# Double-width conversion chunks, turned tiles right behind the score mixing, and two-bank score copies in a one-core attention and feed-forward kernel

## The chip, the cores and the metric

The kernel runs on one core of a Trainium2 chip. The metric is the device time of one execution in microseconds (us), lower is better. The engines are TensorE (PE; its weight loads are PEld), VectorE (DVE), ScalarE (ACT), GpSimd (POOL) and SyncE (SP), which here issues the transfers.

## What is computed

Attention with heads mixed before and after the softmax ("talking heads"), for 4 batches, 12 heads, 448 rows and 64 columns a head, and behind it a feed-forward layer on 1792 rows of 768 with 2048 hidden columns. The weights `w_in` and `w_out` come as 64-bit floats.

```python
scores = scale * np.matmul(q, k.transpose(0, 1, 3, 2))
scores = np.einsum('bhij,hg->bgij', scores, w_pre)
scores = scores - np.max(scores, axis=-1, keepdims=True)
attn = np.exp(scores)
attn = attn / (np.sum(attn, axis=-1, keepdims=True) + 1e-09)
attn = np.einsum('bhij,hg->bgij', attn, w_post)
x = np.matmul(attn, v)          # then rows of all heads side by side
h = x @ w_in
g = where(h >= 1, h, where(h <= -1, 0, (h + 1) ** 2 / 4))
out = g @ w_out
```

## The kernel before

**Tiles and groups.** Each batch's 448 query rows are cut into tiles of 120, 120, 120 and 88, 16 tiles in all. A tile's rows are cut into blocks of 10 (or 9), so that 10 rows times 12 heads fill 120 partitions, and the blocks of a tile into three groups of 4 (of 3 in the tiles of 88). There are 48 groups. The main loop at the end makes one step for each group, with one or two steps more.

**A step.** Step n works on group n, finishes group n-1, and prepares later tiles:

- `load_s`: SyncE moves the blocks of group n+1 out of the tile's scores `ssb` into tiles `s`, with rows and heads side by side on partitions.
- `pre` (L218): TensorE mixes the heads, `ps_l <- s, wpre`. Every second block is a "split" block, which `split` (L209) has cut into a rounded high part `sh` and a rest `sl` on VectorE, for three fast matmuls; the others run as plain fp32.
- `row_max` (L229) on VectorE, `exps` (L233) on ScalarE with the row sums in `sm`; `norm` (L239) adds 1e-9, takes the reciprocal on VectorE, and GpSimd scales `w_post` by it for each block (`wr`).
- `visit` runs `pv` (L300), the product with the values for an earlier tile, into the pair of banks `ps_q`, and `post_rest`; `post` (L256) mixes the exponentials of group n-1 with `wr` into `ps_a`, and ScalarE copies them to `aT`.
- `trans_k` (L137) and `trans_q` (L154) turn raw keys and queries with TensorE into `ps_k` and `ps_t`; a copy rounds them to the high part (`kh`, `qh`), and VectorE subtracts for the rest (`kl`, `ql`). Queries of a tile are turned in two steps of three; keys of the next batch, two pairs of heads a step, in the three steps 6 to 8, 18 to 20 and 30 to 32.
- `scores` (L167) multiplies queries and keys for a tile that comes later, two pairs of heads in a call: the first pair of heads goes into `ps_q`, the second into two banks of the pool `ps_l`; four copies then bring the four banks to `ssb`, the first bank of each pair on ScalarE, the second on VectorE.

**Banks.** Six banks of accumulation memory rotate under the tag "l" for `ps_l`, `ps_k`, `ps_t`, `ps_r`, `ps_a` and the `ps_s` of `scores`; the pair `ps_q` is one pair only, used by `pv` and `scores` in turn.

**The conversion.** Beside the attention, 64 chunks of the 64-bit weights (128 partitions x 384 numbers) are turned into 32-bit floats. `conv_units` lists the work of a chunk in slots: a load into `wraw`, two ScalarE instructions (`scaled` L366 and `lowest` L372), two VectorE instructions (a shift L375 and the sign L381), one GpSimd add (L385), and a store to `wsd` or `wod`, from which the feed-forward part reads later. Units are spread evenly over steps 2 to 42, some in the middle of a step (ahead of `post`) and the rest at its end:

```python
convs(share * (n - NC + 0.4))
...
convs(share * (n - NC + 1))
```

**The order** is written out by hand (a manual schedule): each engine runs its instructions in the order in which the loop calls them, and the waits between engines follow from tiles and slots. SyncE's queue is in order too. In a step SyncE has `load_s` first, then what the conversion, `load_q`, `load_k`, `load_v` and `store_x` issue.

**The feed-forward part** begins in the last four steps and takes some 421 us. It keeps operands at fixed places in areas of memory ("xa", "xc", "xd"); `TEMP` are two scratch places of `gate` and `SUM` one of `sum_w`.

## Time and profile before

| | us |
|---|---|
| median of 3 runs | 884.15 (883.63 to 886.98) |
| the profiled execution | 888.73 |
| its span, first to last instruction | 887.0 |
| TensorE busy in the span | 861.9 (97%) |
| VectorE busy | 681.5 (77%) |
| ScalarE busy | 553.9 (62%) |
| GpSimd busy | 178.7 (20%) |
| attention part, steps 0 to 43 | 24.32 to 437.12 |

The profile gives each instruction's start and length by engine. TensorE's matmuls are pipelined, and the ends in the profile are modelled, so a busy TensorE can still be slowed; what a step really costs is seen from the start of one step's first `ps_l` matmul to the next one's. Where an engine stood idle, the profile names what released it, and the chain of waits follows the work that ended last back from the end. TensorE's granted clock is full (1.00) in nearly all stretches. The line numbers are those of the kernel above.

### The profile page before, as it was taken

Reading aid. Unit: us, or ns where it says so; the run is one execution under the profiler, and the core shown is the slowest. Engines: PE = TensorE matmul, PEld = TensorE weight load, DVE = VectorE, ACT = ScalarE, POOL = GpSimd, SP = SyncE. Lnnn points to the kernel's source line nnn. Section 1 sums busy time; section 2 is a strip of 40 time slices with the busy share of each in tenths; the row PEclk is TensorE's granted clock in tenths of the full one; section 3 lists DMA queues with packets and bytes.
Section 4 is the critical chain, followed back from the end, with each engine's and each line's share of the span. In section 5 each row is a group of like instructions: output and inputs, shape, how many; then the busy total and the mean of one; then the engine's idle time right before and its main releaser. Section 6 shows DMA issues by size and latency. Waiting matters only on the chain.

```text
span 887.0 us, 20352 instructions
## 1 busy us (share of the span) xinstructions
PE 861.9 (97%) x7850; PEld 732.4 (83%) x7850; DVE 681.5 (77%) x1123; ACT 553.9 (62%) x1208; POOL 178.7 (20%) x253
## 2 busy tenths in 40 slices
PE   8999999999999999999999999999999999999998
PEld 6677678767777766777778788889999999999998
DVE  4887778877788787888668877898667987777853
ACT  4786588766776867687766566676667535433431
POOL 0333344543344344435220000000000000000000
PEclk9999999999999999999999999999999999999999
DMA  6758778976788788686375744674444453124341
GB/s 159 227 180 226 201 224 257 279 209 207 234 235 265 227 208 244 208 259 215 121 229 160 255 167 151 206 224 136 128 126 160 135 187 134 54 64 133 97 135 62
DMA packets 160453, 162.50 MB, mean 183 GB/s; under 512 B 67941, under 2 KB 154085, under 8 KB 160357
## 3 DMA queue, kind: packets, MB, share of 16 engines
q1 hardware_dynamic: 157524, 160.51, 59.2%
q8 instruction: 62, 1.02, 0.5%
q10 hardware_dynamic: 2832, 0.69, 0.4%
q14 instruction: 35, 0.28, 0.1%
HBM read 88.81 MB, written 33.82 MB: 138 GB/s over the span
## 4 chain that ended last, share of the span: by engine, by line
PE 72%; DVE 9%; ACT 9%; DMA 7%; issue 2%; SPq 1%; POOL 0%; DVEq 0%; ACTq 0%
PE ps_f L753 23%; PE ps_f L588 23%; PE ps_a L264 7%; PE ps_l L227 5%; DMA s<-ssb 4%; ACT e L236 4%; PE ps_q L315 3%; PE ps_l L225 3%; PE ps_q L182 2%; DVE ssb L191 2%; PE ps_s L182 2%; DVE wt L381 2%; ACT aT L266 2%; PE ps_r L280 1%; DVE wt L375 1%
## 5 line engine op out<-in xcount | busy, mean ns | idle before, releaser
L247 POOL TENSOR_SCALAR wr<-wpost,rs 120x120 f32<-120x120 f32 x180 | 114.3, 650 | 260.2 <-DVE rs L243 186.6
L236 ACT ACTIVATE e<-ps_l,nm 120x448 f32<-120x448 f32 x180 | 111.8, 632 | 74.6 <-DVE nm L230 74.4
L264 PE MATMUL ps_a<-wr,e 120*64 120x120 f32 (+1 forms) x2160 | 119.2, 266 | 0.2 <-ACT e L236 0.2
L264 PEld LDWEIGHTS ps_a<-wr,e 120*64 120x64 f32 x2160 | 110.1, 137 | 3.3 <-issue 2.6
L736 ACT ACTIVATE sgh_p<-gq_p 128x1024 fp32r<-128x1024 f32 (+1 forms) x56 | 53.2, 952 | 90.5 <-PE ps_f L753 90.3
L230 DVE TENSOR_REDUCE nm<-ps_l 120x1 f32<-120x448 f32 x180 | 100.9, 615 | 4.6 <-PE ps_l L227 3.9
L480 DVE SCALAR_TENSOR_TENSOR wl<-wi,wh 128x768 fp32r<-128x768 f32 x71 | 67.7, 954 | 41.9 <-ACT wh L477 41.3
L227 PE MATMUL ps_l<-s,wpre 120*120 120x448 f32 x196 | 95.3, 570 | 4.2 <-DMA s<-ssb 3.0
L753 PE MATMUL ps_f<-wh,sgh_p 128*128 128x384 f32 x294 | 98.2, 334 | 0.0
L753 PE MATMUL ps_f<-wh,sgl_p 128*128 128x384 f32 x294 | 98.2, 334 | 0.0
L753 PE MATMUL ps_f<-wl,sgh_p 128*128 128x384 f32 x294 | 98.2, 334 | 0.0
L477 ACT ACTIVATE wh<-wi 128x768 fp32r<-128x768 f32 x71 | 59.7, 842 | 58.0 <-DVE wi L700 18.0
L737 DVE TENSOR_TENSOR sgl_p<-gq_p,sgh_p 128x1024 fp32r<-128x1024 f32 (+1 forms) x56 | 60.9, 1089 | 35.7 <-ACT sgh_p L736 35.7
L266 ACT ACTIVATE aT<-ps_a 128x360 f32<-128x360 f32 x180 | 73.5, 502 | 4.6 <-PE ps_a L264 3.0
L385 POOL TENSOR_TENSOR wt<-wt,wk 128x384 int32<-128x384 int32 x64 | 64.4, 1013 | 27.4 <-ACT wk L372 14.4
L214 DVE CAST sh<-s 120x448 fp32r<-120x448 f32 (+1 forms) x82 | 31.1, 379 | 41.0 <-DMA s<-ssb 40.9
L225 PE MATMUL ps_l<-sh,wpre_h 120*120 120x448 f32 (+1 forms) x82 | 58.4, 712 | 1.3 <-DVE ql L165 1.3
L215 DVE TENSOR_TENSOR sl<-s,sh 120x448 fp32r<-120x448 f32 (+1 forms) x82 | 54.1, 660 | 2.8
L753 PEld LDWEIGHTS ps_f<-wh,sgl_p 128*128 128x128 f32 x294 | 55.2, 188 | 0.0
L753 PEld LDWEIGHTS ps_f<-wl,sgh_p 128*128 128x128 f32 x294 | 55.2, 188 | 0.0
L753 PEld LDWEIGHTS ps_f<-wh,sgh_p 128*128 128x128 f32 x294 | 55.2, 188 | 0.0
L315 PE MATMUL ps_q<-aT,v 128*64 128x120 f32 (+1 forms) x960 | 55.2, 264 | 0.0
(237 smaller groups left out, 2002.0 us busy)
## 6 DMA issues: line engine op xcount, KB each, us to landing
s<-ssb SPq DMA_DIRECT2D x172, 210.0 KB
wraw<-in_moe_w_in_dram SPq DMA_DIRECT2D x32, 384.0 KB
wraw<-in_moe_w_out_dram SPq DMA_DIRECT2D x32, 384.0 KB
wi<-wod SPq DMA_DIRECT2D x29, 384.0 KB
wi<-wsd SPq DMA_DIRECT2D x28, 384.0 KB
wsd<-wt SPq DMA_DIRECT2D x32, 192.0 KB
wod<-wt SPq DMA_DIRECT2D x32, 192.0 KB
wi<-wss SPq DMA_DIRECT2D x16, 384.0 KB
```

Source lines behind the costliest of these rows:

```text
L225: nc.tensor.matmul(out=lps[m], lhsT=w[:k], rhs=y[:k], start=(j == 0), stop=(j == 2))
L227: nc.tensor.matmul(out=lps[m], lhsT=wpre[:k], rhs=x[:k], start=True, stop=True)
L230: nc.vector.tensor_reduce(out=nm, in_=lps[m], axis=AX.X, op=ALU.max, negate=True)
L236: nc.scalar.activation(out=e, in_=ps, func=AF.Exp, bias=nm, accum_out=sm[:, j:j + 1])
L247: nc.gpsimd.tensor_scalar_mul(out=w[:, :, :ni], in0=wpost[:, :, :ni], scalar1=rs[:, j:j + 1])
L264: nc.tensor.matmul(out=ps[half[s], r, :ni * H], lhsT=e[:, c0:c0 + 64], rhs=w[:, :, :ni], start=True, stop=True)
L266: nc.scalar.activation(out=a[:, :, :, c:c + ni], in_=ps[:, :, :ni * H].rearrange("q r (h i) -> q r h i", h=H), func=AF.Copy)
L315: nc.tensor.matmul(out=to[m][half[s], :n], lhsT=x[:, 2 * m + s, r * D:(r + 1) * D], rhs=a[:, r, 4 * g + 2 * m + s, :n], start=False, stop= ...
L385: nc.gpsimd.tensor_tensor(out=st["t"], in0=st["t"], in1=st.pop("k"), op=ALU.add)
L480: nc.vector.scalar_tensor_tensor(out=lo, in0=t, scalar=2.0 ** -8, in1=hi.bitcast(F32), op0=ALU.mult, op1=ALU.subtract)
L588: nc.tensor.matmul(out=o, lhsT=u[:, c, k], rhs=x, start=first and r == 0 and m == 0, stop=r == 2 and m == 2, skip_group_check=True)
L753: nc.tensor.matmul(out=o, lhsT=x[:, f, c], rhs=y[:, f % 2, :], start=first and f == 0 and m == 0, stop=hf == 1 and f == 3 and m == 2, skip ...
```

## The change

**The conversion** gets 32 chunks of 768 numbers in place of 64 of 384, one in a step, in the steps of the list `CS`: 2 to 42 without 7 to 9, 19 to 21 and 31 to 33, the steps in which keys are turned. The load of step n+1's chunk is issued in step n behind the query and key loads; ScalarE's `conv_scaled` stands behind the exponentials, the other four instructions (`conv_rest`) behind `post`, and the store of step n-1's chunk behind those. `wraw` has 2 slots for 3, `wt` 3 for 4, `wk` 1 for 2, each of twice the size; `s10` has 8 slots for 10, `sh` and `sl` 2 for 3.

**Turned tiles.** Queries and keys are turned one step number later than before, but right behind `pre` and not behind `post`; their copies come behind the exponentials and `norm`. The high part of the keys is copied by ScalarE throughout. Loads of raw queries and keys go from the end of a step to the place behind the transposes.

**Scores.** VectorE copies the two banks of `ps_q` with one instruction; ScalarE copies the two `ps_s` banks.

**norm**: GpSimd adds the 1e-9. **gate**: `TEMP` and `SUM` lie elsewhere, with a second pair of `TEMP` places for the later gates.

```diff
@@ trans_k
+        def out():
+            hi, lo = kt[b, hp]
+            nc.scalar.activation(out=hi, in_=ps, func=AF.Copy)
+            nc.vector.tensor_tensor(out=lo, in0=ps, in1=hi.bitcast(F32), op=ALU.subtract)
+
         def rest():
             nc.tensor.transpose(out=ps[:, SM:], in_=y, identity=i)
-            hi, lo = kt[b, hp]
-            if b:
-                nc.vector.tensor_copy(out=hi, in_=ps)
-            else:
-                nc.scalar.activation(out=hi, in_=ps, func=AF.Copy)
-            nc.vector.tensor_tensor(out=lo, in0=ps, in1=hi.bitcast(F32), op=ALU.subtract)
+            return out
         return rest
@@ scores
-        for h, x in todo:
-            nc.scalar.activation(out=ssb[t][:n, h, :], in_=x[:n], func=AF.Copy)
-
-        def copies():
-            for h, x in rest:
-                nc.vector.tensor_copy(out=ssb[t][:n, h, :], in_=x[:n])
-        return copies
+        h = 2 * hps[0]
+        nc.vector.tensor_copy(out=ssb[t][:n, h:h + 2, :], in_=wide[:n, :, :S])
+        for s in range(2):
+            nc.scalar.activation(out=ssb[t][:n, 2 * hps[1] + s, :], in_=ps[1][s][:n], func=AF.Copy)
@@ load_s, split
-        x = ap_.tile([KM, S], F32, tag="s10", name="s10", bufs=10)
+        x = ap_.tile([KM, S], F32, tag="s10", name="s10", bufs=8)
-        hi = ap_.tile([KM, S], F32R, tag="sh", name="sh", bufs=3)
-        lo = ap_.tile([KM, S], F32R, tag="sl", name="sl", bufs=3)
+        hi = ap_.tile([KM, S], F32R, tag="sh", name="sh", bufs=2)
+        lo = ap_.tile([KM, S], F32R, tag="sl", name="sl", bufs=2)
@@ norm
-        nc.vector.tensor_scalar_add(out=rs[:, :k], in0=sm[:, :k], scalar1=1e-9)
+        nc.gpsimd.tensor_scalar_add(out=rs[:, :k], in0=sm[:, :k], scalar1=1e-9)
@@ the conversion (convert and conv_units are gone)
+    CS = [n for n in range(2, NG - 5) if not any(x <= n < x + 3 for x in (3 * t - 5 for t, y in enumerate(tiles)
+                                                                          if t and y[1] == 0))]
+    def conv_load(i):
+        craw[i] = qp.tile([128, 2 * CW], I64, tag="wraw", name="wraw", bufs=2)
+        src = conv_ends(i)[0]
+        nc.sync.dma_start(out=craw[i] if i % 2 else craw[i].rearrange("p (k f) -> p k f", f=128), in_=src)
+    def conv_scaled(i):
+        cwt[i] = qp.tile([128, 2 * CW], I32, tag="wt", name="wt", bufs=3)
+        nc.scalar.activation(out=cwt[i].bitcast(F32), in_=halves(i)[1].bitcast(F32), func=AF.Copy,
+                             scale=2.0 ** -111)
+    def conv_rest(i):
+        lo, hi = halves(i)
+        t = cwt[i]
+        k = qp.tile([128, 2 * CW], I32, tag="wk", name="wk", bufs=1)
+        nc.scalar.activation(out=k, in_=lo.bitcast(U32), func=AF.Copy, scale=2.0 ** -29)
+        nc.vector.tensor_single_scalar(out=t, in_=t, scalar=3, op=ALU.logical_shift_left)
+        nc.vector.scalar_tensor_tensor(out=t, in0=hi, scalar=-0x80000000, in1=t,
+                                       op0=ALU.bitwise_and, op1=ALU.bitwise_or)
+        nc.gpsimd.tensor_tensor(out=t, in0=t, in1=k, op=ALU.add)
+    def conv(n, f):
+        if n in CS and CS.index(n) < 2 * NF:
+            f(CS.index(n))
@@ scratch places
-    SUM = ("xd", 29504)
-    TEMP = (("xd", 32576), ("xd", 36672))
+    SUM = ("xd", 37696)
+    TEMP = tuple(tuple(("xd", x + 4096 * i) for i in range(2)) for x in (29504, 30720))
@@ the loop's tables
-                    at.setdefault(3 * t - 6 + g + (t == 2), []).append(lambda t=t, g=g: trans_q(t, g))
+                    w0 = 3 * t - 5 + g + (t == 2)
+                    at.setdefault(w0, []).append(lambda t=t, g=g: trans_q(t, g))
-                        put(3 * t - 7 + hp // 2, lambda nb=nb, hp=hp: load_k(nb, hp))
-                        at.setdefault(3 * t - 6 + hp // 2, []).insert(0, lambda nb=nb, hp=hp: trans_k(nb, hp))
+                        w0 = 3 * t - 5 + hp // 2
+                        mid.setdefault(w0 - 1, []).append(lambda nb=nb, hp=hp: load_k(nb, hp))
+                        at.setdefault(w0, []).insert(hp % 2, lambda nb=nb, hp=hp: trans_k(nb, hp))
@@ the loop
             for m in ms:
                 pre(m)
             nxt = list(groups[n + 1][1::2]) if n + 1 < NG else []
+            turned = [f() for f in [f() for f in at.pop(n, ())]]
+            for f in mid.pop(n, ()):
+                f()
+            conv(n + 1, conv_load)
             for m in ms:
                 row_max(m, nm[:, m - ms[0]:m - ms[0] + 1])
...
-            for f in copies:
-                f()
+            conv(n, conv_scaled)
             if ms:
                 norm(ms, sm)
+            for f in (*turned, *copies):
+                f()
             for m in nxt:
                 split(m)
-            convs(share * (n - NC + 0.4))
             if n == NG:
                 step(0)
             for m in old:
                 post(m)
-            for f in [f() for f in at.pop(n, ())]:
-                if f:
-                    f()
+            conv(n, conv_rest)
+            conv(n - 1, conv_store)
             if not early:
                 for f in visit(n, rests):
                     f()
-            for f in [scores(t, hps) for t, hps in vis.pop(n, ())]:
-                f()
+            for t, hps in vis.pop(n, ()):
+                scores(t, hps)
             for f in late.pop(n, ()):
                 f()
-            convs(share * (n - NC + 1))
```

VectorE where the first keys of the second batch are turned; `sh`/`sl` are splits, `wt` the conversion's shift and sign, `nm` the row maxima. Before, from the end of step 6 to the maxima of step 7:

```order
L375 TENSOR_SCALAR wt<-wt 128x384
L381 SCALAR_TENSOR_TENSOR wt<-wraw,wt 128x384
L165 TENSOR_TENSOR ql<-ps_t,qh 128x360
L148 CAST kh_1236<-ps_k 128x448
L151 TENSOR_TENSOR kl_1237<-ps_k,kh_1236 128x448
L148 CAST kh_1242<-ps_k 128x448
L151 TENSOR_TENSOR kl_1243<-ps_k,kh_1242 128x448
L191 COPY ssb<-ps_q 88x448
L191 COPY ssb<-ps_s_1270 88x448
L375 TENSOR_SCALAR wt<-wt 128x384
L381 SCALAR_TENSOR_TENSOR wt<-wraw,wt 128x384
L230 TENSOR_REDUCE nm<-ps_l 120x1 x4
```

After, step 7 from its maxima to those of step 8:

```order
L222 TENSOR_REDUCE nm<-ps_l 120x1 x4
L206 CAST sh<-s_1233 120x448
L207 TENSOR_TENSOR sl<-s_1233,sh 120x448
L235 RECIPROCAL rs<-rs 120x4
L146 TENSOR_TENSOR kl_1256<-ps_k,kh_1255 128x448
L146 TENSOR_TENSOR kl_1262<-ps_k,kh_1261 128x448
L166 TENSOR_TENSOR ql<-ps_t,qh 128x360
L206 CAST sh<-s_1235 120x448
L207 TENSOR_TENSOR sl<-s_1235,sh 120x448
L183 COPY ssb<-ps_q 88x896
L222 TENSOR_REDUCE nm<-ps_l 120x1 x4
```

The conversion and the casts of `kh` are gone from between two sets of maxima, the subtractions follow the step's own maxima, and one copy of 896 columns takes the place of two.

SyncE, the step that follows. Before, from the store behind step 7's `post` through its end to the loads of the scores `s`:

```order
L412 DMA wsd<-wt 128x384
L125 DMA qraw<-in_q_dram 120x6x64
L115 DMA kraw<-in_k_dram 128x3x64 x2
L116 DMA kraw<-in_k_dram 64x2x64
L115 DMA kraw<-in_k_dram 128x3x64 x2
L116 DMA kraw<-in_k_dram 64x2x64
L347 DMA xd<-xo 768x1x120
L405 DMA wraw<-in_moe_w_in_dram 128x3x128
L412 DMA wsd<-wt 128x384
L206 DMA s_1486<-ssb 120x1x448
```

After, from the query load of step 7 to the first load of step 8:

```order
L124 DMA qraw<-in_q_dram 120x6x64
L114 DMA kraw<-in_k_dram 128x3x64 x2
L115 DMA kraw<-in_k_dram 64x2x64
L114 DMA kraw<-in_k_dram 128x3x64 x2
L115 DMA kraw<-in_k_dram 64x2x64
L380 DMA wsd<-wt 128x2x384
L339 DMA xd<-xo 768x1x120
L198 DMA s_1405<-ssb 120x1x448
```

One store and one load of the conversion have gone from between the key loads and the score loads; the score loads (`s`) now follow the store of `xo`.

VectorE in a step without keys and with a conversion. Before, step 5 from the reciprocal to the maxima of step 6:

```order
L242 TENSOR_SCALAR rs<-sm 120x4
L243 RECIPROCAL rs<-rs 120x4
L214 CAST sh<-s_960 120x448
L215 TENSOR_TENSOR sl<-s_960,sh 120x448
L375 TENSOR_SCALAR wt<-wt 128x384
L381 SCALAR_TENSOR_TENSOR wt<-wraw,wt 128x384
L191 COPY ssb<-ps_q 88x448
L191 COPY ssb<-ps_s_1087 88x448
L375 TENSOR_SCALAR wt<-wt 128x384
L381 SCALAR_TENSOR_TENSOR wt<-wraw,wt 128x384
L230 TENSOR_REDUCE nm<-ps_l 120x1 x4
```

After, step 5 from its maxima to the score copy:

```order
L222 TENSOR_REDUCE nm<-ps_l 120x1 x4
L206 CAST sh<-s_937 120x448
L207 TENSOR_TENSOR sl<-s_937,sh 120x448
L235 RECIPROCAL rs<-rs 120x4
L166 TENSOR_TENSOR ql<-ps_t,qh 128x3x88
L206 CAST sh<-s_939 120x448
L207 TENSOR_TENSOR sl<-s_939,sh 120x448
L373 TENSOR_SCALAR wt<-wt 128x768
L374 SCALAR_TENSOR_TENSOR wt<-wraw,wt 128x768
L183 COPY ssb<-ps_q 88x896
```

The two pairs of conversion instructions of 384 stood on both sides of the score copies and ahead of the maxima; now one pair of 768 stands ahead of the one wide copy.

## Rows read from the trace of the kernel before

**Rows 1.** Windows of steps: from:to, length, engine busy (instructions), TensorE clock, DMA share, GB/s.

```profile
51.51:60.89 9.38, 9.38 (x124) 7.39 (x122) 6.82 (x15) 7.73 (x22) 4.44 (x7) 1.00 0.71 218
60.89:69.86 8.97, 8.97 (x120) 6.95 (x119) 7.22 (x16) 7.22 (x20) 3.95 (x6) 1.00 0.52 171
69.86:80.08 10.22, 10.22 (x132) 8.23 (x130) 6.83 (x16) 7.70 (x21) 2.05 (x3) 1.00 0.73 218
80.08:114.78 34.70, 32.14 (x374) 23.50 (x374) 26.59 (x56) 21.05 (x59) 13.51 (x20) 0.95 0.77 207
184.71:195.94 11.23, 10.28 (x131) 8.25 (x130) 6.84 (x14) 8.55 (x23) 2.70 (x5) 1.00 0.86 232
195.94:229.65 33.71, 30.57 (x373) 22.79 (x373) 27.15 (x58) 19.96 (x57) 13.77 (x20) 1.00 0.75 210
311.91:346.11 34.20, 30.86 (x375) 22.74 (x374) 27.27 (x58) 20.92 (x59) 13.26 (x20) 1.00 0.81 219
114.78:184.71 69.93, 69.90 (x908) 53.95 (x906) 59.06 (x127) 55.73 (x155) 32.17 (x43) 1.00 0.81 251
229.65:301.67 72.02, 70.08 (x908) 53.92 (x906) 59.22 (x127) 55.97 (x155) 32.37 (x43) 1.00 0.81 244
346.11:419.15 73.04, 70.85 (x908) 54.01 (x906) 59.54 (x127) 55.16 (x154) 33.24 (x45) 1.00 0.75 231
```

**Rows 2.** Chain of waits, steps 8 to 10: start us, us, what.

```profile
97.14 5.79 DMA s<-ssb
...
115.79 0.61 PE ps_l L225 x3
```

**Rows 3.** Timeline of VectorE, steps 8 and 9: start, us, line, operation, [idle before, releaser].

```profile
92.04 0.61 DVE L148 CAST kh<-ps_k 128x448 fp32r<-128x448 f32 x1
...
96.34 2.21 DVE L230 TENSOR_REDUCE nm<-ps_l 120x1 f32<-120x448 f32 x4
102.95 0.39 DVE L214 CAST sh<-s 120x448 fp32r<-120x448 f32 x1 [4.40 <-DMA s<-ssb]
...
107.56 0.61 DVE L191 COPY ssb<-ps_q 120x448 f32<-120x448 f32 x1
```

**Rows 4.** Timeline of SyncE's DMA issues, step 8.

```profile
90.94 1.27 SPq L115 DMA_DIRECT2D kraw<-in_k_dram  x2
...
97.14 2.58 SPq L206 DMA_DIRECT2D s<-ssb  x3
```

**Rows 5.** Who waited for whom, whole run: us in total, times, longest.

```profile
DVE sh L214 <- DMA s<-ssb: 40.9, 28, 4.4
```

**Rows 6.** The same for SyncE's DMA queue.

```profile
SPq L405 <- DVE wt L381: 37.0, 20, 7.4
```

**Rows 7.** Single lines: ns min/median/max, first and last start, forms.

```profile
L375 DVE TENSOR_SCALAR wt<-wt x64: 346/350/1218, 49.6 to 417.7; 128x384 int32<-128x384 int32 x64
...
L381 DVE SCALAR_TENSOR_TENSOR wt<-wraw,wt x64: 557/559/1250, 50.0 to 418.0; 128x384 int32<-128x384 int32 x64
...
L385 POOL TENSOR_TENSOR wt<-wt,wk x64: 991/1002/1122, 51.6 to 419.6; 128x384 int32<-128x384 int32 x64
...
L242 DVE TENSOR_SCALAR rs<-sm x48: 158/164/171, 29.4 to 464.6; 120x4 f32<-120x4 f32 x36, 120x3 f32<-120x3 f32 x12
...
L247 POOL TENSOR_SCALAR wr<-wpost,rs x180: 550/583/990, 29.8 to 466.5; 120x120 f32<-120x120 f32 x172, 120x108 f32<-120x108 f32 x8
```

**Rows 8.** Groups by line: busy us, mean ns of one, idle before.

```profile
L236 ACT ACTIVATE e<-ps_l,nm 120x448 f32<-120x448 f32 x180 | 111.8, 632 | 74.6 <-DVE nm L230 74.4
...
L480 DVE SCALAR_TENSOR_TENSOR wl<-wi,wh 128x768 fp32r<-128x768 f32 x71 | 67.7, 954 | 41.9 <-ACT wh L477 41.3 <-DMA wi<-wsd 0.6
...
L477 ACT ACTIVATE wh<-wi 128x768 fp32r<-128x768 f32 x71 | 59.7, 842 | 58.0 <-DVE wi L700 18.0 <-PE ps_f L588 16.8 <-DVE wi L513 14.1
...
L215 DVE TENSOR_TENSOR sl<-s,sh 120x448 fp32r<-120x448 f32 (+1 forms) x82 | 54.1, 660 | 2.8
```

**Rows 9.** DMA issues: queue, count, KB each.

```profile
wraw<-in_moe_w_in_dram SPq DMA_DIRECT2D x32, 384.0 KB
```

More of the change, by code (lines that the diff above doesn't have):

```diff
@@ L608, in tile_talking_heads_moe, with gate @@
     maxima = deque()
-    def gate(src, dst, act):
+    def gate(src, dst, act, end):
         a = dst
@@ L613, in gate @@
             n = src.shape[2]
-            a = view("ga", *TEMP[ngate[0] % 2], 2, n)
+            a = view("ga", *TEMP[end][ngate[0] % 2], 2, n)
             ngate[0] += 1
@@ L929, in tile_talking_heads_moe @@
         later(NG + 1, lambda: x_sums(2), sx("B22", 2, 2))
-        def convs(goal):
-            while conv and nconv - len(conv) < goal:
-                conv.popleft()()
         for n in range(NG + 2):
@@ L944, in tile_talking_heads_moe @@
                 s_ss.close()
-            share = nconv / (NE - 1 - NC)
             ms = groups[n] if n < NG else ()
```

123 lines of the change are left out of this document (36 added, 87 removed).

## The prediction

> **What bounds the kernel now.** I cut the attention part at the starts of its steps (a step is one pass of the main loop; step n begins with the first `ps_l` matmul of group n). TensorE is busy for 69.90 of the 69.93 us of steps 10 to 17 [rows 1], so time can be won only where it waits or is slowed. Step 4 takes 9.38 us; step 5, the same work without the transposes of half the queries, 8.97, so these cost 0.41; step 6, which also turns two pairs of keys, takes 10.22 [rows 1]. That is what a step costs when TensorE sets its length. Step 8 is step 6 without query transposes, so 9.81 is due; step 9 turns no keys and has one split block less, three matmuls of together 0.61 [rows 2], so 9.38 - 0.61 = 8.77. Steps 7 to 9 are due 10.22 + 9.81 + 8.77 = 28.80 and took 34.70; the same steps of the next two batches took 33.71 and 34.20; step 18, a twin of step 6, took 11.23 [rows 1]. Lost: 5.90 + 4.91 + 5.40 + 1.01 = **17.2 us**.
>
> Between the batches stand eight steps of equal work: 10 to 17 took 69.93, 22 to 29 took 72.02, 34 to 41 took 73.04 [rows 1]. Against the quietest, 2.09 + 3.11 = **5.2 us** are lost. So 22.4 us is what the change can give back in the attention part; in the feed-forward part no instruction is moved, only two scratch places.
>
> Why are the steps late? In step 8 VectorE begins at 92.04 with casts of keys that were turned a step before, gets to its row maxima only at 96.34, then stands 4.40 us, until 102.95, for the block that it has to split, and its score copy comes at 107.56 [rows 3]. SyncE issued that block at 97.14, behind key loads that begin at 90.94 [rows 4] and behind a load and a store of the conversion; the chain of waits shows 5.79 us from there to its arrival [rows 2]. Over the run VectorE waits 40.9 us for such blocks [rows 5], and SyncE itself stands 37.0 us before conversion loads, with score loads queued behind [rows 6].
>
> **The change, part by part.**
>
> *Conversions out of the turned steps.* Before, 64 chunks ran at 64/41 = 1.6 a step in every step. After, 32 of double width, none in steps 7 to 9, 19 to 21, 31 to 33, and none is loaded one step earlier, where key loads now are. A turned step loses 1.6 x (0.35 + 0.56) = 1.5 us of VectorE [rows 7] and three or four SyncE issues of about 0.6 (a key load's is 1.27/2 [rows 4]).
>
> *kh to ScalarE.* Two casts of 0.61 [rows 3] a turned step leave VectorE: 1.2 us. ScalarE gains about as much but loses its conversions there.
>
> *Score copies.* Per call, one two-bank copy on VectorE for two of 0.61 [rows 3]: at most 1.22 after, at least 0.61 (no price for the second bank); I take 1.06, nearer the first, since the columns double. It waits for six matmuls alone, no longer for ScalarE's copy of the neighbouring bank, so the pair `ps_q` comes free some 0.6 earlier. The five calls ahead of the loop could give 5 x 0.16 = 0.8; counted at nothing, for the range alone.
>
> *Order in a step.* Row maxima come first on VectorE and score loads first on SyncE, with no conversion store ahead of them that waits for GpSimd's newest add. VectorE then has in a turned step: four maxima 2.21, two splits of 0.39 [rows 3] + 0.66 [rows 8], two `kl` and a `ql` of at most 0.61 each, a wide copy 1.06, a reciprocal 0.2: 7.4 us under a step of 10.2. So these steps should run at TensorE's pace. I leave a quarter of the 17.2 as lost still, since in steps 8, 20 and 32 the score loads are those of a new tile and can't be issued before the last copies of the step ahead: **-13**.
>
> *The ordinary steps, now with a chunk of 768.* The longest chain through VectorE and ScalarE goes from one step's first maximum to the next one's: the first maximum 0.6 and four exponentials of 0.63 [rows 8] 3.1, scaling 0.84 [rows 8], `qh` and `ql` at most 0.61 each, taken 1.0 for both, second split 1.05, shift, sign, wide copy 1.06. The shift of 768 lies between 0.35 (all of it fixed) and 0.70, the sign between 0.56 and 1.12 [rows 7]; the nearest row, another VectorE instruction with two tensors and a scalar over 128x768, has 0.954 [rows 8], so I take 0.55 and 0.95. Sum 8.55 against 9.38 for such a step: 0.8 to spare. TensorE needs the result later still: the pair `ps_q` only after `pre` and transposes, some 3 us into the step, while the wide copy ends about 1 us into it. So the cover is 0.8 on VectorE and some 2 on TensorE; only what exceeds both is lost at once. Since nothing here waits for a slot or a store any more, I expect two thirds of the 5.2 back: **-3.5**.
>
> *The sum's add on GpSimd.* One VectorE instruction of 0.164 becomes one on GpSimd, for which VectorE's reciprocal waits, with `ql`, the second split and the shift queued behind it. Between 0.16 and 0.58 (GpSimd's scaling of 120 elements) [rows 7]; taken 0.4, as the engine is the same as the latter's. Hidden, since `ql` waits for ScalarE longer than that; without that cover 0.4 of the 0.8 is gone, and still nothing lost.
>
> *Transposes.* They come one step number later, but behind `pre` and not behind `post`, so their copies end within the step. Steps 2 and 3 use their queries within it, with no attention product in between: up to 0.5 each, **+0.8** together. The accumulation bank that they take earlier costs nothing: with keys the query transposes wait for the first exponential, due some 2 us into the step, and are reached past 3. *Fewer slots* (8 for 10, 2 for 3): `pre` frees them at the start of the step, nothing. *TEMP and SUM*: the same instructions in the same order, nothing.
>
> Sum: -13 - 3.5 + 0.8 = -15.7. The profiled execution took 888.73 (span 887.0, 1.7 around it), so 873.0 by it; it lies 4.6 above the median of 884.15, and I carry the difference over to the median: **868.5**.
>
> **The rivals.** *Score loads stay late.* Steps 10 to 17 moved 251 GB/s at a DMA share of 0.81 [rows 1], so 310 would be all. There a chunk was 384 KB loaded [rows 9] and half of that stored, 576 x 1.6 = 900 KB a step; now it is 1152 KB in 8.7 us, 29 GB/s more, and 280 on the mean; where values are loaded too (steps 13 to 15, 25 to 27, 37 to 39) it comes to the limit. If the queue doesn't empty there, blocks come later each time, by at most the 1 us that the cover leaves over: 9 x 0.8 = 7 us of the gain go: **875.5**. Against it: the loads are now issued earlier in a step.
>
> *The stall only changes its name.* Six key loads still stand on SyncE ahead of the next step's score loads. If they, and not the conversion, made the blocks late, VectorE's wait stays and only its leftovers go; perhaps 3 us in all: **881**, no change by measure. Against it: step 6 issues key loads too and lost nothing.
>
> *GpSimd's add blocks VectorE* (slower). Shift and sign have medians of 0.350 and 0.559 but maxima of 1.218 and 1.250, and GpSimd's add lasts 1.002 [rows 7]: a VectorE instruction at times stands for nearly a whole add. The add of 768 takes some 2.0. Where it meets a shift or a split in each of 32 steps, the chain of 8.55 grows by up to 1.7 to 10.25, 0.9 beyond the step: 32 x 0.9 = 29 lost against 15.7 gained: **897**. It decides from 0.8 + 15.7/32 = 1.3 us of blocking in each step. Against it: the add now starts as a step ends and runs while VectorE copies from PSUM and takes maxima; the plain copies and casts from PSUM in [rows 3] took 0.61 each. The Trainium skill, "SBUF — State Buffer", section "Who interferes with whom", gives the cause: the two engines share a port pair which one instruction holds until it ends. By that rule a meeting costs twice as much with twice the width, and the time would be the rival's; the maxima agree with it, but the meeting itself isn't in the new order.
>
> **How the numbers follow.** Forecast (860.5 to 872) 0.57; late score loads (872 to 879.7) 0.20; the stall renamed (879.7 to 888.6) 0.11; slower by the add 0.12. The floor is all 22.4 and the 0.8 at the start: 861.0, rounded down. For 8 in 10 the range runs from 860.5 through the second case and the third's price: 882. Half a percent, 4.4 us, is about what a measurement of this kernel can tell from no change. Faster 0.77, same 0.11, slower 0.12.
>
> **What would show it.** Right: steps 7 to 9, 19 to 21 and 31 to 33 together at some 90 us for the 102.6 of before; VectorE's wait for score blocks well under 40; no SyncE wait before conversion loads; steps 10 to 17 still at 70 with chunks of twice the width. Wrong: ordinary steps of 10 us with a shift or split of over 1.5 (the add); value-loading steps with late blocks at a DMA share near 1 (the loads); turned steps still of 11 to 12 with VectorE idle before a split (the name). The whole forecast falls if SyncE still issues a step's first score load 3 to 5 us into it.

## The result and the profile after

The changed kernel takes 878.23 us (median of 7 runs, 872.66 to 880.44); the kernel before took 886.98 beside it (7 runs, 883.63 to 890.03). The ratio is 0.9893, with an interval of 0.9856 to 0.9929: faster by 1.1%, where 1.8% was forecast. The profiled execution took 878.23 (span 876.5), against 888.73 (887.0) before.

Windows of the kernel after, from one step's first `ps_l` matmul to another's: steps 7 to 9, 19 to 21 and 31 to 33 (keys are turned), then 13 to 15, 25 to 27 and 37 to 39 (the next batch's values are loaded), then steps 0 to 43. Columns as in [rows 1]; the busy times are those of TensorE, its weight loads, VectorE, ScalarE and GpSimd.

```profile
81.49:111.26 29.77, 29.77 (x384) 24.01 (x382) 19.12 (x35) 21.56 (x55) 10.58 (x17) 1.00 0.76 217
192.40:222.17 29.77, 29.77 (x383) 24.02 (x381) 18.89 (x34) 21.66 (x55) 11.02 (x18) 1.00 0.72 210
306.33:336.23 29.90, 29.90 (x384) 24.00 (x382) 19.84 (x36) 21.41 (x55) 12.02 (x18) 1.00 0.77 219
135.36:165.00 29.64, 26.75 (x363) 21.16 (x361) 20.98 (x41) 22.52 (x57) 17.00 (x19) 1.00 0.92 267
247.43:278.28 30.85, 26.69 (x361) 21.13 (x361) 21.36 (x43) 21.20 (x55) 17.49 (x19) 1.00 0.92 251
360.33:390.07 29.74, 26.71 (x362) 21.15 (x361) 21.04 (x41) 22.34 (x57) 16.95 (x19) 1.00 0.91 265
27.23:426.65 399.42, 387.97 (x4974) 304.43 (x4972) 291.68 (x532) 311.23 (x776) 203.99 (x243) 1.00 0.80 231
```

In the turning steps TensorE is now busy from end to end: 89.4 us for nine steps that took 102.6 [rows 1]. In the value-loading steps it stands still for 2.9, 4.2 and 3.0 us, at a DMA share of 0.91 to 0.92. The 44 steps take 399.4 us (412.8 before). The loop starts later, at 27.23 instead of 24.32, so step 44 begins 10.5 us earlier, and that is the whole difference of the spans.

Step 14, which begins at 144.30, shows how a value-loading step loses. SyncE's issues in the kernel after (timeline):

```profile
140.07 2.40 SPq L130 DMA_DIRECT2D v<-in_v_dram  x1
142.52 2.12 SPq L133 DMA_DIRECT2D v<-in_v_dram  x2
145.49 4.08 SPq L198 DMA_DIRECT2D s<-ssb  x4
```

The chain of waits there (start, us, what):

```profile
140.07 10.41 DMA v<-in_v_dram
```

VectorE's timeline in the same step:

```profile
151.64 0.39 DVE L206 CAST sh<-s 120x448 fp32r<-120x448 f32 x1 [3.69 <-DMA s<-ssb]
...
153.12 0.19 DVE L326 COPY xo<-ps_q 128x36 f32<-128x36 f32 x1
```

And TensorE's:

```profile
153.36 0.47 PE L180 MATMUL ps_q<-kh,qh 64*120 64x448 f32 x2 [1.46 <-DVE xo L326]
```

The value load is issued at 140.07 and takes 10.41 us to land; the score loads behind it are issued from 145.49, and the block to be split arrives at 151.64. VectorE has waited 3.69 us for it, and behind the split stands the small copy that empties the pair `ps_q`, for which TensorE waits 1.46 us.

The waits of the kernel after, over the whole run (us in total, times, longest):

```profile
DVE sh L206 <- DMA s<-ssb: 59.4, 38, 4.4
...
PE ps_q L180 <- DVE xo L326: 9.5, 6, 2.3
```

The same for SyncE's queue:

```profile
SPq L357 <- DVE wt L374: 2.8, 4, 1.1
```

VectorE's wait for score blocks has grown from 40.9 [rows 5] to 59.4 us; SyncE's wait for VectorE before conversion loads has shrunk from 37.0 [rows 6] to 2.8.

### The profile page after: what moved, and what is told of

The parts are those of the page before. It is cut to its first block, busy times and chain, and to the rows that moved or that the text cites. A ratio compares the mean times of both kernels' runs of the same rounds, so it can differ in the third digit from the quotient of the medians.

```text
span 876.5 us, 19947 instructions
## 1 busy us (share of the span) xinstructions
PE 854.6 (97%) x7850; PEld 736.4 (84%) x7850; DVE 644.6 (74%) x945; ACT 563.5 (64%) x1162; POOL 213.9 (24%) x269
## 4 chain that ended last, share of the span: by engine, by line
PE 84%; DMA 9%; DVE 3%; ACT 2%; SPq 1%; issue 1%; ACTq 0%
PE ps_f L711 23%; PE ps_f L546 21%; PE ps_a L256 10%; PE ps_l L219 8%; PE ps_q L307 5%; PE ps_l L217 5%; DMA s<-ssb 4%; PE ps_q L180 3%; PE ps_s L180 3%; DMA v<-in_v_dram 2%; PE ps_r L272 2%; PE ps_q L302 1%; DMA k<-in_k_dram 1%; PE ps_k L141 1%; DMA wraw<-in_moe_w_in_dram 1%; PE ps_t L161 1%
## 5 line engine op out<-in xcount | busy, mean ns | idle before, releaser
L239 POOL TENSOR_SCALAR wr<-wpost,rs 120x120 f32<-120x120 f32 x180 | 142.1, 805 | 64.0 <-DVE rs L235 47.4
L222 DVE TENSOR_REDUCE nm<-ps_l 120x1 f32<-120x448 f32 x180 | 105.0, 619 | 13.6 <-PE ps_l L219 10.4
L258 ACT ACTIVATE aT<-ps_a 128x360 f32<-128x360 f32 x180 | 79.9, 493 | 13.3 <-PE ps_a L256 4.7
L206 DVE CAST sh<-s 120x448 fp32r<-120x448 f32 (+1 forms) x82 | 32.5, 396 | 59.4 <-DMA s<-ssb 59.4
L183 DVE COPY ssb<-ps_q 120x896 f32<-120x896 f32 (+1 forms) x48 | 52.1, 1085 | 29.6 <-PE ps_q L180 29.6
L185 ACT ACTIVATE ssb<-ps_s 120x448 f32<-120x448 f32 (+1 forms) x96 | 47.1, 544 | 28.7 <-PE ps_s L180 26.6
L376 POOL TENSOR_TENSOR wt<-wt,wk 128x768 int32<-128x768 int32 x32 | 58.2, 1820 | 6.7 <-ACT wk L372 6.7
```

The source lines that it names most:

```text
L222: nc.vector.tensor_reduce(out=nm, in_=lps[m], axis=AX.X, op=ALU.max, negate=True)
L239: nc.gpsimd.tensor_scalar_mul(out=w[:, :, :ni], in0=wpost[:, :, :ni], scalar1=rs[:, j:j + 1])
L258: nc.scalar.activation(out=a[:, :, :, c:c + ni], in_=ps[:, :, :ni * H].rearrange("q r (h i) -> q r h i", h=H), func=AF.Copy)
```

## The experiments

Two measures are used. The steps are cut as above, so each run is read from its own trace; "nine turned" and "nine value" are the sums of the windows shown above for the kernel after (89.4 and 90.2 us), and a heavy step is one of these eighteen. And "the loop", the 44 steps, is given net of the clock, which is an estimate: in some stretches TensorE's granted clock was 0.5 (1.2 of 2.4 GHz), and in slices of 4 us the length times one minus the clock is taken off (1.7 us for before, nothing for after). Net, the loop takes 411.1 us before and 399.4 after. Every run has one trace; the kernel after and runs 2, 3, 6, 7 and 8, which differ little, spread over some 397 to 400 by this measure.

**1. No value loads in batches 1 to 3.** The kernel leaves them out and uses the values of batch 0 again.

```diff
-put(w0, lambda t=t, g=g: load_v(tiles[t + 1][0], g))
+put(w0, lambda t=t, g=g: vt.update({(tiles[t + 1][0], g): vt[0, g]}))
```

> Leaves out the value loads of batches 1 to 3 (batch 0's values are used again), so 9 transfers of 384 KB and 18 of 32 KB less; every engine's order stays. In the kernel after, steps 14, 15, 26, 27, 38 and 39 lie 10.5 us above their own PE-bound length, and there TensorE waits for VectorE's small copy of xo (L326), which stands behind a split that waits for a score load. Theory T (transfers: the score loads are late because value loads and double-width chunks are queued ahead of them): the 10.5 us go, VectorE's wait for score loads falls from 59.4 to about 45 us, step 44 starts 9 to 10.5 us earlier. Theory O (it is VectorE's order alone, or VectorE slowed by the 1.8 us GpSimd adds): the six steps keep over 7 of the 10.5 us.

Measured: 867.75 us (ratio 0.978, 0.9756 to 0.9804). The nine value steps take 82.2, the loop 390.2. VectorE's wait:

```profile
DVE sh L206 <- DMA s<-ssb: 46.0, 36, 3.5
```

Theory T holds in the main, theory O falls: with VectorE's order untouched, 8 of the 10.5 us go with the transfers. Some 2.5 stay in steps 14, 15 and 38 without a value load, so those loads are not the whole of it.

**2. Value loads behind the next step's score loads.**

```diff
-put(w0, lambda t=t, g=g: load_v(tiles[t + 1][0], g))
+mid.setdefault(w0 + 1, []).append(lambda t=t, g=g: load_v(tiles[t + 1][0], g))
```

> One edit on the kernel after: each value load is issued behind the next step's score loads instead of ahead of them; bytes and engine orders stay. Theory T-queue (what makes the scores late is what stands ahead of them in the queue): the six value steps lose 6 to 10 of their 10.5 us, the wait for score loads falls by over 8 us. Theory T-bytes (the stretch is at the limit of the transfers, whatever their order; windows there show 0.83 to 0.98 DMA share): at most 4 us go, the lateness moves to the next step's scores or to the conversions' loads. Theory O: nothing changes (within 1 us).

Measured: 877.82 us (0.9861 to 0.9935), as the kernel after. The nine value steps fall by 5.3 to 84.9, but the loop takes 398.6 net, 0.8 less: the loss went to later steps. TensorE in step 17 of this run (timeline):

```profile
181.73 0.44 PE L180 MATMUL ps_s<-kh,qh 64*88 64x448 f32 x2 [1.74 <-DVE ql L166]
```

In the value steps the 5.3 lie between the theories (at most 4 by T-bytes, 6 to 10 by T-queue); the loop decides for T-bytes: moving a transfer in the row mostly moves the lateness. The Trainium skill, "DMA: Bandwidth & Descriptors", section "Queues, rings and completion order", says that each transfer engine takes descriptors from a row in its order. The run agrees: of the 5.3 us that the value steps got back, the rest of the loop paid 4.5.

**3. The small copy of xo on ScalarE.**

```diff
-                    if t + 1 < len(tiles):
-                        nc.vector.tensor_copy(out=x, in_=y)
-                    else:
-                        nc.scalar.activation(out=x, in_=y, func=AF.Copy)
+                    nc.scalar.activation(out=x, in_=y, func=AF.Copy)
```

> One edit on the kernel after: the 36-column copy of xo (nine of 185 ns on VectorE) goes to ScalarE, right behind the larger copy of the same product, so it no longer stands behind the split that waits for scores. Theory P (the path runs late scores, split, xo copy, TensorE; the scores themselves would be in time for TensorE's own use of them): score loads stay as late (VectorE's wait near 59 us), and TensorE's idle behind the xo copy, 9.5 us, goes: step 44 starts 7 to 10 us earlier. Theory L (the scores are too late for TensorE itself): TensorE waits at the next step's ps_l for sh or sl instead, and under 4 us go.

Measured: 877.14 us (0.9841 to 0.9932); the loop 400.3 net. TensorE's own waits in this run:

```profile
PE ps_l L219 <- DMA s<-ssb: 8.6, 7, 2.3
```

Theory L: with the copy out of the way, TensorE waits for score blocks themselves, and the loop is no shorter. The late block is the cause, the copy only the place where it showed.

**4. The nine free steps are the value-loading ones.**

```diff
-any(x <= n < x + 3 for x in (3 * t - 5 for t, y in enumerate(tiles)
+any(x <= n < x + 3 for x in (3 * t + 1 for t, y in enumerate(tiles)
...
```

> One edit on the kernel after: the nine steps without a conversion are the value-loading ones (13 to 15, 25 to 27, 37 to 39) instead of those that turn keys (7 to 9, 19 to 21, 31 to 33), which get one each. By theory T the value steps' 10.5 us go almost whole. What the turned steps (now at their PE-bound length, 29.8 us for three) then show tells which part of the change gave their 17 us back: if it was the missing conversions, 4 to 6 us come back in each batch (12 to 17 us in all, step 44 starts 2 to 7 us later); if it was the lead of the transposes and kh on ScalarE, under 2 us in each batch, and step 44 starts 5 to 10 us earlier.

Measured: 874.10 us (0.9832 to 0.9887). First three turned steps and first three value steps of this run:

```profile
78.60:112.73 34.13, 30.21 (x383) 24.00 (x381) 22.82 (x41) 25.24 (x60) 16.66 (x19) 1.00 0.88 246
136.84:163.37 26.53, 26.53 (x363) 21.13 (x361) 18.63 (x37) 19.01 (x50) 12.52 (x18) 1.00 0.71 220
```

The nine value steps fall by 10.7 us to 79.6, TensorE's pace; the nine turned ones rise by 10.9 to 100.3. The loop is at 396.9 net. Neither of the two cases expected holds whole: net of the clock 4.4, 2.9 and 2.8 us come back in the three batches (of the 10.9, some 1 us is the clock, 0.97 in the last three), mostly between the "4 to 6" of the missing conversions and the "under 2" of the other parts. A whole conversion in each turned step thus brings back some 10 of their 17 us, and not all. A turned step has key loads as large as a value step's value loads (448 KB), and it comes to the same: three heavy steps in a row with whole conversions on top lose 2.8 to 4.4 us here, 3.1 to 4.3 in the value steps of the kernel after.

**5. Half a chunk in each heavy step.**

```diff
...
+    for n in range(2, NG - 5):
+        if n in TURN + VAL:
+            if not part:
+                i = todo.pop(0)
+                part = [(i, 0, 1), (i, 1, 1)]
+            CU[n] = part.pop(0)
+        elif todo:
+            CU[n] = (todo.pop(0), 0, 2)
...
```

> Spreads the same conversions otherwise, on the kernel after: the 9 key-turning and the 9 value-loading steps get half a chunk each (384 columns), the 23 others a whole one (768), so 23 + 9 = 32. By bytes a value-loading step then moves 576 KB less than in the kernel after, a turning step 576 KB more than there and 576 KB less than in the run with one conversion in each turning step. Theory T-bytes (any step with 448 KB of keys or values and a whole chunk is beyond what the transfers carry in its length): the value steps lose 8 of their 10.1 us, the turned ones gain 0 to 3, step 44 starts 5 to 9 us earlier than after's 426.65 (less what the clock took at the start), time 868 to 873 us. Rival (a conversion costs by being there, by its number of loads and stores in SyncE's row, not by its bytes): 41 conversion steps for 32, the turned steps lose 6 to 11 us as with whole chunks and the value steps keep 5 or more; time 876 to 885.

Measured: 863.46 us (median of 5, 863.00 to 867.96), ratio 0.9776 (0.9753 to 0.9799), beyond the forecast of the theory and faster than both kernels. First turned three, first value three, and the loop:

```profile
78.59:109.01 30.42, 29.98 (x383) 24.01 (x381) 21.61 (x41) 23.97 (x61) 14.15 (x20) 1.00 0.81 228
133.12:159.64 26.52, 26.52 (x362) 21.12 (x360) 22.00 (x44) 20.84 (x56) 16.51 (x22) 1.00 0.87 266
24.40:411.70 387.30, 386.73 (x4973) 304.78 (x4971) 298.87 (x550) 320.05 (x794) 206.79 (x252) 1.00 0.82 238
```

TensorE idles 0.6 us in 387.3: hardly any wait is left to win in the loop. The number of conversions does not decide (41 steps here have one, 32 in the kernel after). Half a chunk halves the engines' work in a heavy step as well as the bytes; that the bytes are what counts rests on run 1, which took away transfers and no engine's work.

**6 to 8. Three parts undone singly:** kh of later batches cast by VectorE, four score copies of one bank, the sums' add on VectorE.

```diff
-            nc.scalar.activation(out=hi, in_=ps, func=AF.Copy)
+            if b:
+                nc.vector.tensor_copy(out=hi, in_=ps)
+            else:
+                nc.scalar.activation(out=hi, in_=ps, func=AF.Copy)
...
-        nc.vector.tensor_copy(out=ssb[t][:n, h:h + 2, :], in_=wide[:n, :, :S])
-        for s in range(2):
-            nc.scalar.activation(out=ssb[t][:n, 2 * hps[1] + s, :], in_=ps[1][s][:n], func=AF.Copy)
+        for hp, x in zip(hps, ps):
+            nc.scalar.activation(out=ssb[t][:n, 2 * hp, :], in_=x[0][:n], func=AF.Copy)
+        for hp, x in zip(hps, ps):
+            nc.vector.tensor_copy(out=ssb[t][:n, 2 * hp + 1, :], in_=x[1][:n])
...
-        nc.gpsimd.tensor_scalar_add(out=rs[:, :k], in0=sm[:, :k], scalar1=1e-9)
+        nc.vector.tensor_scalar_add(out=rs[:, :k], in0=sm[:, :k], scalar1=1e-9)
```

> Undoes one part: in batches 1 to 3 kh is cast by VectorE again (18 casts of some 0.61 us), all else as after. A whole conversion put into each turned step cost those steps 10.9 us in an earlier run, of the 15.7 that the change gave back there. Theory K (the other 4.8 us are kh's): the turned steps are 3 to 6 us above their PE-bound length. Theory N (VectorE has room: 1.2 us more in a step of 10.2 of which it fills some 6): under 1 us in the nine steps, time within 3 us of the kernel after.

> Undoes one part: four copies of one bank each for a score call, ScalarE the first of each pair, VectorE the second (96 of some 0.615 us for 48 of 1.085), all else as after. The prediction counted the wide copy's gain as hidden in ordinary steps. Theory H (hidden): step 44 within 1.5 us of the kernel after, apart from what the clock takes. Theory W (the pair of banks comes free earlier by the wide copy, which shortens the path behind late scores): the value steps lose another 2 to 5 us, step 44 starts 2 to 5 us later.

> Undoes one part: the add of 1e-9 to the sums goes back to VectorE (48 of 164 ns there for 48 of 272 ns on GpSimd), all else as after. The prediction called it hidden. Theory H (hidden): step 44 within 1 us of the kernel after, apart from what the clock takes. Rival G (it puts VectorE's reciprocal, and ql, splits and shift behind it, behind a busy GpSimd): the value steps lose 1 to 3 us less than the 10.1 of the kernel after.

Measured: 876.24 (0.9884 to 0.9917), 875.39 (0.9867 to 0.9939) and 875.11 us (0.9862 to 0.9915). The loops, net: 397.4, 398.5, 397.7, each 1 to 2 below the kernel after, and the nine value steps, net of the clock, spread over 87 to 90 in these runs and after. The nine turned ones stay at 89.5, 89.3 and 89.7. So N for kh and H for the other two: none of the three parts has a gain that these runs can tell from nothing.

**9 and 10. The distribution alone, on the kernel before.**

```diff
...
+        part = [0 if n in turn else 1 if n in val else 1 for n in range(NE - 1)]
+
+        def goal(n, f):
+            return nconv * (sum(part[NC:n]) + f * sum(part[n:n + 1])) / sum(part[NC:])
...
-            share = nconv / (NE - 1 - NC)
...
-            convs(share * (n - NC + 1))
+            convs(goal(n, 1))
```

Run 10 has 0.5 for the turned and the value steps. Both also take up a first share already in step 0, and steps 0 to 6 take 61.8 and 63.2 us for 55.8; what follows uses steps 7 to 43.

> One edit on the kernel before: its conversion units are paced by the step, none taken up in steps 7 to 9, 19 to 21 and 31 to 33 (where its 15.9 us above the PE-bound length lay), the same share in the 32 others; chunk size, order, copies, kh and sums stay. Theory D (the distribution is the whole of the change's effect): those nine steps fall to under 3 us above their length, the value-loading steps rise from 5.3 to 9 or 11, step 44 starts 8 to 12 us earlier, time 875 to 880 us. Theory M (the order of each step, with the transposes ahead, is worth the 4.8 us that a conversion put back into the turned steps of the kernel after did not take): the nine steps keep 4 to 8 us, step 44 starts 2 to 8 us earlier, time 880 to 886.

> As the run beside it, but the 9 key-turning and the 9 value-loading steps each take half the conversion units of the 23 others: the sharing of the best run so far (863.5 us), on the kernel before. Theory D: the loop's steps come to within 5 us of their PE-bound length, time 864 to 869 us. Theory M: 5 to 10 us stay in the steps after the turned ones, time 870 to 876. If neither (over 878), then the double-width chunk, loaded early in a step, is needed for the sharing to help.

Measured: 901.82 us (1.0108 to 1.0201) and 890.49 (1.0022 to 1.0061). Neither theory foresaw this: D is out, and M expected a gain in both. From step 7 on run 9 loses 6.2 us against the kernel before, and run 10 gains 4.1 (the table below). So sharing by halves helps without the double-width chunk too, other than the third case expected of run 10. SyncE's wait in run 9, over the whole run:

```profile
SPq L405 <- DVE wt L381: 65.2, 19, 11.9
```

SyncE's issues in its step 14, which began at 154.17:

```profile
157.32 1.11 SPq L405 DMA_DIRECT2D wraw<-in_moe_w_out_dram  x1
158.52 3.43 SPq L206 DMA_DIRECT2D s<-ssb  x4
```

The wait before conversion loads has grown from 37.0 [rows 6] to 65.2 us (from step 7 on from 29.6 to 54.4), and the score loads queued behind are issued 4.4 us into the step, where the kernel after issues them 1.2 into its step 14. The sum of these waits is no price by itself: run 10 has 47.2 from step 7 on and is shorter there than the kernel before.

**11. The change with an even distribution** (32 conversions over the 41 steps).

```diff
-    CS = [n for n in range(2, NG - 5) if not any(...)]
+    CS = [2 + (41 * i + 20) // 32 for i in range(32)]
```

> One edit on the kernel after: its 32 conversions lie evenly over the 41 steps 2 to 42, whatever else a step does, as in the kernel before (7 of the 9 key-turning steps and 7 of the 9 value-loading steps have one). Order in a step, copies, kh, sums and chunk size stay as after. Theory B (order and distribution are both needed; the new order keeps a late block from growing, but a heavy step with a whole chunk still is beyond its transfers): 7 to 9 us in the turned steps, 4 to 8 in the value steps, step 44 starts 1 to 5 us later than in the kernel after, apart from the clock; time 876 to 884. Theory C (the distribution does nothing by itself, the order all, as the two runs on the kernel before suggest): turned and value steps together stay at 10 us or less, time 870 to 877.

Measured: 873.71 us (0.9791 to 0.9890). First turned and second value three:

```profile
81.61:111.94 30.33, 29.99 (x384) 24.01 (x382) 21.02 (x38) 24.43 (x58) 12.41 (x16) 1.00 0.88 238
245.86:274.17 28.31, 26.58 (x363) 21.13 (x361) 20.33 (x40) 21.50 (x54) 16.84 (x20) 1.00 0.88 256
```

Theory C: the nine turned steps take 92.8, the nine value steps 82.1, the loop 393.0, which is 6.4 less than in the kernel after. Seven of nine turned steps have a conversion and lose 3.3 us together, where nine of nine in run 4 lost 10.9. It may be that a late block is carried over between neighbouring heavy steps and that one step without a conversion lets this drain; that is not shown. The turned steps fit it (2.0 us lost in 19 to 21, which have one each, 0.6 and 0.8 in the other threes, each with one step free), the value steps don't (0 and 1.8 with one step free, 0.7 with none).

With runs 5 and 9 to 11 the two halves of the change, the distribution and the rest, can be taken apart. Steps 7 to 43, us, net of the clock (the new order has one more turning of keys in this stretch, 1.2 us of TensorE):

| | even | none in turned steps | half in heavy steps |
|---|---|---|---|
| order and chunks of before | 355.3 | 361.5 (run 9) | 351.2 (run 10) |
| order and chunks of after | 338.6 (run 11) | 345.2 (after) | 333.1 (run 5) |

Down each column the new order with its chunks gives 16 to 18 us. Along each row "none where keys are turned" costs 6 to 7 us, and half a chunk in the heavy steps gives 4 to 6. Each cell is one trace; the kernel after and runs 2, 3, 6, 7 and 8 lie between 343.1 and 345.4 in this stretch, so the differences are clear of that spread.

**12. One slot for raw weights**, on the kernel of run 5, so that a conversion's load must wait again.

```diff
-        craw[i, c] = qp.tile([128, 2 * CW], I64, tag="wraw", name="wraw", bufs=2)[:, :w * CW]
+        craw[i, c] = qp.tile([128, 2 * CW], I64, tag="wraw", name="wraw", bufs=1)[:, :w * CW]
```

> One edit on the best kernel so far (half a chunk in each heavy step, 863.5 us): one slot for raw weights in place of two, so that a conversion's load waits on SyncE until VectorE is done with the step's own chunk, and the next step's score loads are queued behind it, as in the kernel before. Theory S (that wait, not the bytes, is what made the distribution useless on the kernel before): SyncE's wait before conversion loads rises from under 10 us to 30 or more, score loads are issued 3 us or more into the step, steps lie 10 to 40 us above their length in all, time 875 to 905 us. Rival (the wait is short or the loads in time all the same): under 5 us, time 863 to 868.

Measured: 940.10 us (1.0567 to 1.0625). SyncE's wait over the run:

```profile
SPq L371 <- DVE wt L388: 159.0, 35, 7.0
```

VectorE's:

```profile
DVE sh L206 <- DMA s<-ssb: 149.2, 44, 6.0
```

SyncE's issues in step 6, which began at 78.80:

```profile
80.52 0.40 SPq L371 DMA_DIRECT2D wraw<-in_moe_w_in_dram  x1
80.97 0.53 SPq L394 DMA_DIRECT2D wsd<-wt  x1
81.54 3.61 SPq L198 DMA_DIRECT2D s<-ssb  x4
```

Theory S, beyond its range (10 to 40 us): the slot alone costs 77 us at the same bytes and the same distribution. In this run's waits the granted clock fell often, 18.8 us by the slices in the loop; net, the loop takes 447.0 for run 5's 387.3, so 60 us remain. The load goes out only when VectorE is done with the step's own chunk, so the score loads behind it go out 2.7 us into a step that needs them early. How much of the 60 is theirs is not taken apart: ScalarE waits 23.2 us for the conversion's own loads too.

## Why the prediction was right, and where it was not

**What bounds the kernel: right.** TensorE idles 11.5 us of 399.4 in the kernel after, 10.1 of it in steps 14, 15, 26, 27, 38 and 39, behind late score blocks. Another 1.1 us lies at the end of step 24, and the trace puts it down to ScalarE's copy of `ps_s`. The kernel after, TensorE and VectorE:

```profile
247.43 0.98 PE L219 MATMUL ps_l<-s,wpre 120*120 120x448 f32 x2 [1.09 <-ACT ssb L185]
...
244.48 0.39 DVE L206 CAST sh<-s 120x448 fp32r<-120x448 f32 x1 [2.71 <-DMA s<-ssb]
```

The same matmul and the same copy in run 5:

```profile
240.94 1.01 PE L219 MATMUL ps_l<-s,wpre 120*120 120x448 f32 x2
...
241.05 0.98 ACT L185 ACTIVATE ssb<-ps_s 120x448 f32<-120x448 f32 x2
```

There the matmul begins before that copy, so it does not wait for it. The other thing that it waits for is the transfer of its score block, and VectorE had just stood 2.71 us for a block of the same group: a late block here too, as far as the trace tells.

**Conversions out of the turned steps, the term of -13: right in place and near in size, wrong in cause.** Steps 6 to 9, 18 to 21 and 30 to 33 took 134.3 us together and take 116.4. Of the 17.9 between them, 1.2 are three turnings of queries that now lie in other steps, so 16.7 of the 17.2 us that the prediction found lost came back, 3.7 more than taken. The quarter kept as lost for the score loads of a new tile was hardly needed. But the prediction made it the merit of the missing conversions. In run 11, with conversions in seven of the nine turned steps, these lose only 3.3 us, so at an even distribution most comes back with the conversions in place (with whole ones in all nine, run 4, some 10 us are lost). Taking them all out gives those 3.3 us and costs the value steps 8.1, and in the table it costs 6 to 7 us on either order. What gives lies in what the two rows of the table differ in. Run 12 and SyncE's wait (37.0 to 2.8) point at the order in SyncE's row, score loads ahead and conversion loads that find a free slot, but that part was not run by itself. The prediction had it in view ([rows 6], "score loads queued behind") but put it down as a part, not as the half that carries all.

**The ordinary steps, the term of -3.5: failed.** Against run 5, where steps 10 to 17, 22 to 29 and 34 to 41 take 69.1 each, the kernel after needs 72.2, 75.2 and 72.4: 12.6 us lost. Before took 215.0 in the three [rows 1], after takes 219.8, of which 1.2 is one turning of queries more in each. The failing step is "since nothing here waits for a slot or a store any more, I expect two thirds of the 5.2 back": it took the stalls of before for waits on slots, and left out that 32 chunks on 32 steps put 28% more bytes of conversion (41/32) on a value step than 32 on 41 would. The price of the prediction's own first rival, "score loads stay late", was 9 x 0.8 = 7 us in just these nine steps; measured, against run 5, are 10.7, at a DMA share of 0.91 to 0.92. The rival took 310 GB/s for the limit; the blocks were late at 251 to 267. Its mechanism is shown by runs 1, 2 and 4. That rival should have been the forecast for these steps, beside the gain in the turned ones.

**The signs that the prediction named.** Right ones: the nine turned steps at 89.4 (some 90 was named), no wait of length before conversion loads. Wrong ones, and they are those of the first rival: VectorE's wait for score blocks at 59.4 instead of well under 40, steps 10 to 17 at 72.2 instead of 70, and late blocks at a DMA share of 0.92 in value steps. VectorE's wait in total was a poor sign, though: in run 5 it is 46.7, more than before, and TensorE loses 0.6 us; there no single wait is longer than 2.8, against 4.4 before and after. Run 5's line:

```profile
DVE sh L206 <- DMA s<-ssb: 46.7, 38, 2.8
```

**kh, the wide copy, the add: right that they are hidden**, as far as runs 6 to 8 can tell. The prices were good: for the wide copy 1.06 taken and 1.085 measured; for the chunk of 768 the shift was taken at 0.55 and the sign at 0.95, and the medians below are 0.553 and 0.959.

**GpSimd's add, the slower rival: fell.** Lines L373, L374 and L239 of the kernel after (ns min/median/max):

```profile
L373 DVE TENSOR_SCALAR wt<-wt x32: 546/553/689, 45.6 to 415.0; 128x768 int32<-128x768 int32 x32
...
L374 DVE SCALAR_TENSOR_TENSOR wt<-wraw,wt x32: 957/959/996, 46.2 to 415.6; 128x768 int32<-128x768 int32 x32
...
L239 POOL TENSOR_SCALAR wr<-wpost,rs x180: 548/698/1381, 32.6 to 455.9; 120x120 f32<-120x120 f32 x172, 120x108 f32<-120x108 f32 x8
```

The maxima of 1.218 and 1.250 [rows 7] are gone, though the add now lasts 1.82 us. GpSimd's scaling became slower instead (median 583 [rows 7] to 698, longest 990 to 1381). The Trainium skill, "SBUF — State Buffer", section "Who interferes with whom", says that the order of issue decides which of the two engines is blocked; these lines agree: the long times moved from VectorE's conversion to GpSimd's scaling, for which TensorE waits only once, 0.3 us. That the shared port is the cause here was not tested by a run.

**The start, counted at nothing: missed by 2.9 us, the clock's.** The loop began 2.9 us later, and that is TensorE's clock: at 11.64, after 1.14 us without work (a key load), TensorE went on, and from 12.5 the granted clock was half. Windows of the kernel after:

```profile
12.50:14.00 1.50, 1.50 (x7) 1.03 (x7) 0.62 (x1) 0.83 (x2) 0.00 (x0) 0.54 0.71 125
14.00:16.00 2.00, 2.00 (x10) 1.22 (x10) 1.21 (x2) 0.83 (x3) 0.00 (x0) 0.50 0.71 197
```

In runs 4, 5 and 8 the clock stayed full there, and with the same instructions ahead of it the loop began at 24.40 to 24.49, against 24.32 before. The wide copies gave nothing here, where the prediction allowed up to 0.8 for its range: in run 7, with four copies in each call and a full clock, the loop began at 23.58, 0.8 earlier. That is one trace.

**From 868.5 to 878.2.** By its profile the prediction gave 873.0, and 878.2 came, 5.2 more. The turned steps gave 3.7 us more than taken; the ordinary ones 7.1 less (they took some 3.6 longer, forecast was 3.5 shorter); the start took 2.9; steps 0 to 5 became 0.3 shorter, where 0.8 longer was forecast. That makes the 5.2. The other 4.5 is the carry-over to a median of three runs, 884.15, which lay 2.8 below the median of the seven, these three among them.

By its time the result lies in the stretch that the prediction gave to its first rival (872 to 879.7, chance 0.20) and not in the forecast's (860.5 to 872, chance 0.57). That the time comes so near to this rival's 875.5 is in part luck: the rival's sum held neither the 2.9 us of the start nor the 3.7 that the turned steps gave beyond it, and these two nearly cancel.

**Left open.** The table's 16 to 18 us belong to all that its two rows differ in: the place of loads and of transposes, the chunk's width, and the three parts of runs 6 to 8. The last are excluded singly, and run 12 shows what a slot wait on SyncE can cost; the width, the place of the loads and the transposes' lead were not run apart.

## What to carry to other kernels

When side work is spread over a loop, count the bytes of each step, main transfers and side transfers together, and give the heavy steps less; leaving some out pushes their share into the others, which may be as heavy. Put the transfers that the next step needs first in the issuing engine's row, and let no load stand ahead of them that can wait for a buffer: here one buffer less cost 77 us, some 19 of them by the clock. A stall that a change makes vanish in one place has to be looked for in the place where the moved work went.

## What was not expected of the hardware

Neither the DMA share nor the bytes per second of a stretch tells whether score blocks come late in it. At 0.91 to 0.92 and 251 to 267 GB/s (value steps, kernel after) TensorE stood 2.9 to 4.2 us; at 0.87 and 266 GB/s (run 5) not at all; but at 0.88 and 246 (run 4, turned steps) 3.9 us, and at 0.88 and 256 (run 11, value steps) 1.7. What stands in the row ahead of a block when it is issued is not in these averages. That it decides is the reading of runs 2 and 12; it was not measured block by block.

An idle time can cost twice. In run 8, step 14, TensorE waited 2.61 us for the copy of xo, and then ran at half clock. Its timeline there and in step 26 of the same run:

```profile
152.15 0.73 PE L180 MATMUL ps_q<-kh,qh 64*120 64x448 f32 x2 [2.61 <-DVE xo L326]
...
266.07 0.46 PE L180 MATMUL ps_q<-kh,qh 64*120 64x448 f32 x2 [3.00 <-DVE xo L326]
```

Windows of the first stretch, the clock third from the end:

```profile
152.00:154.00 2.00, 1.85 (x10) 1.63 (x12) 1.93 (x5) 0.00 (x0) 2.00 (x3) 0.50 1.15 260
156.00:158.00 2.00, 2.00 (x5) 1.27 (x4) 0.94 (x2) 0.72 (x2) 1.30 (x1) 0.50 0.72 242
```

The slices of 4 us from 148 to 160 give 3.4 us lost by the clock, more than the wait itself. It doesn't follow each time: in step 26 TensorE waited 3.00 us, and the granted clock stayed at 1.00. After 1.37 us without work at the start the kernel before kept its clock, and after 1.14 the kernel after lost it.
